# First tile's q and k loaded in 1 KB runs and turned by 64x64 products, the last kept sum seeded into PSUM, and a new order

## The chip, the cores and the metric

The kernel runs on one core of a Trainium2 chip. The metric is the device time of one execution in microseconds, the median of several runs; smaller is better. The profile is of one execution, and its times count from the start of its span.

## The reference

Attention in chunks of 64 tokens over 8 batches, 8 heads, 576 tokens and 64 features per head, then a feed-forward block over the 4608 tokens with 512 model and 2048 hidden features. All is float32:

```
scores = (q_c @ k_c.T) / 8                     # per chunk of 64 tokens
attn   = exp(scores - max) / (sum + 1e-9)
out    = attn @ v_c
x = out, heads beside each other               # 4608 x 512
h = x @ w_in                                   # 512 x 2048
g = h if h >= 1, 0 if h <= -1, else (h + 1)^2 / 4
y = g @ w_out                                  # 2048 x 512
```

## The kernel before, in words

The tokens are worked on in nine tiles of 512: the first 512 tokens of each batch, and one tile (the seventh) of the last 64 tokens of all eight. Heads are taken in pairs, four pairs (g = 0 to 3) per tile. Every FFN product is made of three products in the chip's reduced float32 form: high part of x with high and low part of the weight, and low part of x with the high part (`ffn_in`, L777; `ffn_out`, L813; each block of 128 hidden features is 12 products of 512 columns for either). The weights are loaded in 16 blocks for either matrix and split into high and low parts on the chip (`prepare`, L431: three operations on ACT, L442, L445 and L467, two on DVE, L450 and L471).

The first three tiles use the plain form, block by block. The tiles from the fourth on go two by two through a fast scheme for products of 2x2 blocks, with seven products in place of eight (`ffn_quad`, L1115; `ffn_mixed_out`, L1159). It needs mixed weights, which `mix_weights` (L883) makes while the first three tiles run and which POOL's queue writes to DRAM and streams back.

**Head.** Tile 0's attention is done pair by pair. `load_heads` (L527) loads q and k of a pair through `load_rows` (L485): two issues, one per head, in runs of 256 bytes, one token's features each; SP's queue issues them, and ACT's for k of pairs 0 and 1 (L537). A 128x512 tile then holds 64 tokens of a chunk on 64 partitions, for two heads. `attn_turn` (L551) turns it by four 128x128 transposes on PE (`flip`, L544) into a PSUM bank, and ACT copies it to SBUF (L560). `scores_of` and `values_of` (L569, L586) make 32 products of 64x64 each; `attn_softmax` (L647) takes the maximum (L658), subtracts it (L661), takes the exponential on ACT (L664), the sum and its reciprocal on DVE (L669 to L671) and multiplies on POOL (L674). `attn_turn_back` (L678) turns the result by `flip` again, with an ACT copy (L684). `attn_split` (L728) makes the high part xh on ACT (L737) and the low part xl on DVE (L738).

While PE has nothing ready in this head, the planner puts in warm-up products of the identity matrix, `warm` (L1472), until the first FFN product.

**Later pairs.** From tile 1 on, attention goes by two pairs at once in bursts (`burst`, L1390): 128-byte-run loads (`load_blocks`), 32x32 turns on DVE (L565), `attn_softmax_pair` (L686) and four DMAs that swap blocks of the turned result (`move`, L717). `PAIRS` (L1369) lists after which blocks of the first three tiles a burst is placed, `SCHEDULE` (L310) after which blocks, counted from the start, a mix of weights is placed and which scratch it uses.

**Order.** What each engine does is not written down as such: every operation is given to a planner (`Plan.add`, L87) with its engine, an assumed cost, what it reads and writes, and for loads their size and run. `Plan.run` (L153) plays this through as a list scheduler: an engine takes the ready operation of lowest rank. After each of two rounds the ranks are replaced by due times that are counted back from the end (`deadlines`, L123). The third pass writes the instructions in that order, so each engine's stream is fixed beforehand. `first_loads` (L1308) and `load_more` (L1334) give the loads' first ranks.

**Tail.** The last step of the last tile, `ending` in `ffn_mixed_out` (L1192), makes its products in two halves of tokens, e = 0 and 1, and two chunks of features, c = 0 and 1, into four half banks (`last_product`, L1150). They go into a pair of banks for e = 0 that attention used, `a_banks`, and `h_banks` for e = 1. `store_last` (L1222) adds on DVE the sum kept in D (`total_of`, L1065), turns it by 32x32 on DVE (L1239, L1242), and SP's and ACT's queues store it (L1248). Elsewhere (L1182) a kept sum is instead copied by ACT into PSUM, `seeded` (L1077), and the products add to it.

## Time and profile before

| | |
|---|---|
| median of three runs | 792.53 us (792.34 to 794.37) |
| the profiled execution | 793.6 us, its span 791.8 us |
| granted TensorE clock over the span | 0.999 |
| busy: PE, DVE, ACT, POOL | 782.8, 659.9, 523.4, 178.4 us |
| moved by DMA | 177.16 MB, 224 GB/s on average |

How to read it: the span runs from the first instruction to the last; the execution's own time is 1.8 us more than that. PE is TensorE's products (PEld its weight loads beside them), DVE VectorE, ACT ScalarE, POOL GpSimd, SP the engine that only issues DMAs; SPq, ACTq are the queues' issuing instructions. In the timeline a row is one instruction, or several alike in a row with their count (x4), with start, duration, engine, line of the kernel, output <- input, and in brackets the idle time before it and what ended it. A product's duration is from its start to its modelled end, and products overlap, so a row of several is shorter than the sum of its parts.

### The profile page before, as it was taken

What the parts mean: (1) busy time and instruction counts of PE and PEld (TensorE: products, weight loads), DVE (VectorE), ACT (ScalarE), POOL (GpSimd) and SP (SyncE); (2) the same over time, 40 slices, a digit from 0 to 9 for tenths busy, and PEclk for the clock granted to TensorE, in tenths of its full rate; (3) what the DMA queues carried; (4) which work ended last, traced back from release to release, by engine and by line L of the source; (5) the groups of instructions that cost most, each with busy time, mean ns of one, the idle gap of its engine ahead of it and who ended that gap; (6) DMA issues with size and microseconds to landing.
All of it is one profiled execution on the core that took longest, in us unless ns stands there. A gap on an engine that the chain in (4) does not pass through costs nothing.

```text
span 791.8 us, 15101 instructions
## 1 busy us (share of the span) xinstructions
PE 782.8 (99%) x5626; PEld 646.2 (82%) x5626; DVE 659.9 (83%) x1013; ACT 523.4 (66%) x903; POOL 178.4 (23%) x294
## 2 busy tenths in 40 slices
PE   9999999999999999999999999999999999999997
PEld 8788888878878888887887888888888888888886
DVE  4889998898679889998769999887699976755796
ACT  5998975444445456886579667865797658657851
POOL 1000005743234433222111112121112111211211
PEclk9999999999999999999999999999999999999999
DMA  9896869858799867898899879989766896666664
GB/s 207 221 359 152 252 136 289 290 174 234 190 277 278 219 170 232 246 299 229 225 243 240 225 210 271 273 226 241 204 198 185 220 260 207 191 192 191 183 207 106
DMA packets 254664, 177.16 MB, mean 224 GB/s; under 512 B 211968, under 2 KB 220160, under 8 KB 254592
## 3 DMA queue, kind: packets, MB, share of 16 engines
q0 software_dynamic: 33344, 117.98, 47.4%
q1 hardware_dynamic: 216992, 57.18, 32.0%
q10 hardware_dynamic: 4256, 1.05, 0.7%
q8 instruction: 44, 0.72, 0.4%
q14 instruction: 28, 0.23, 0.1%
HBM read 133.17 MB, written 38.80 MB: 217 GB/s over the span
## 4 chain that ended last, share of the span: by engine, by line
PE 83%; DVE 7%; ACT 4%; DMA 3%; SPq 1%; issue 1%; ACTq 0%; DVEq 0%
PE ps_o L1060 39%; PE ps_o L823 14%; PE ps_h L788 14%; PE ps_h L1060 12%; PE ps_a L579 2%; DMA aT_both<-qT_both 2%; PE ps_h L600 1%; DVE big_wo L1111 1%; DMA k_sb_both<-in_k_dram 1%; ACT big_wo L1110 1%; ACT big_wo L1107 1%; DMA words_wi<-in_moe_w_in_dram 1%; SPq L490 1%; SPq L722 0%; PE ps_o L600 0%
## 5 line engine op out<-in xcount | busy, mean ns | idle before, releaser
L968 POOL DMA_DIRECT2D big_wi<-mixed x144 | 76.8, 534 | 325.7 <-PE ps_o L1060 178.2
L788 PE MATMUL ps_h<-xh,parts_wi 128*128 128x512 f32 x376 | 123.9, 392 | 0.1
L823 PE MATMUL ps_o<-parts_wo,gh 128*128 128x512 f32 x384 | 119.5, 392 | 0.0
L1060 PE MATMUL ps_o<-big_wo,big_wi 128*128 128x512 f32 x396 | 95.6, 389 | 0.0
L1060 PE MATMUL ps_o<-gh,big_wi 128*128 128x512 f32 x264 | 88.6, 391 | 0.4 <-ACT big_wo L1075 0.3
L1060 PEld LDWEIGHTS ps_o<-big_wo,big_wi 128*128 128x128 f32 x396 | 74.3, 188 | 15.5
L788 PEld LDWEIGHTS ps_h<-xh,parts_wi 128*128 128x128 f32 x376 | 70.6, 188 | 16.5 <-DVE r L799 1.2
L823 PEld LDWEIGHTS ps_o<-parts_wo,gh 128*128 128x128 f32 x384 | 71.4, 188 | 15.3 <-issue 0.3
L1060 PE MATMUL ps_h<-big_wi,big_wi 128*128 128x512 f32 x312 | 75.9, 390 | 0.0
L823 PE MATMUL ps_o<-parts_wo,gl 128*128 128x512 f32 x192 | 74.8, 390 | 0.0
L788 PE MATMUL ps_h<-xl,parts_wi 128*128 128x512 f32 x188 | 73.3, 390 | 0.1
L1060 PE MATMUL ps_o<-big_wi,big_wi 128*128 128x512 f32 x282 | 70.8, 391 | 0.7 <-ACT tmp L1075 0.4
L1060 PEld LDWEIGHTS ps_h<-big_wi,big_wi 128*128 128x128 f32 x312 | 58.4, 188 | 12.2
L1167 ACT CAST big_wo<-big_wo 128x512 fp32r<-128x512 f32 x76 | 47.2, 622 | 31.6 <-PE ps_o L1060 19.9
L1060 PEld LDWEIGHTS ps_o<-big_wi,big_wi 128*128 128x128 f32 x282 | 52.6, 188 | 12.8 <-ACT tmp L1075 1.3
L1167 ACT CAST gh<-big_wo 128x512 fp32r<-128x512 f32 x76 | 47.2, 621 | 23.2 <-PE ps_o L1060 18.2
L1168 DVE TENSOR_TENSOR big_wo<-big_wo,big_wo 128x512 fp32r<-128x512 f32 x76 | 51.6, 684 | 11.6 <-ACT big_wo L1167 11.6
L1110 ACT ACTIVATE big_wo<-big_wo 128x512 f32<-128x512 f32 x96 | 59.8, 632 | 1.9
L1060 PEld LDWEIGHTS ps_o<-gh,big_wi 128*128 128x128 f32 x264 | 49.5, 188 | 12.0 <-ACT big_xl L753 0.8
L1168 DVE TENSOR_TENSOR gl<-big_wo,gh 128x512 fp32r<-128x512 f32 x76 | 51.6, 683 | 8.6 <-ACT gh L1167 8.5
L795 ACT ACTIVATE r<-ps_h 128x512 f32<-128x512 f32 x47 | 28.1, 597 | 36.4 <-PE ps_h L788 36.2
L1060 PE MATMUL ps_o<-gl,big_wi 128*128 128x512 f32 x132 | 51.4, 390 | 0.0
(269 smaller groups left out, 1648.9 us busy)
## 6 DMA issues: line engine op xcount, KB each, us to landing
big_wi<-mixed POOLq DMA_DIRECT2D x144, 512.0 KB, 4.7
big_wo<-mixed POOLq DMA_DIRECT2D x24, 512.0 KB, 4.3
words_wi<-in_moe_w_in_dram SPq DMA_DIRECT2D x16, 512.0 KB, 7.0
words_wo<-in_moe_w_out_dram SPq DMA_DIRECT2D x16, 512.0 KB, 8.8
v_sb<-in_v_dram SPq DMA_DIRECT2D x60, 128.0 KB, 4.0
q_sb_both<-in_q_dram SPq DMA_DIRECT2D x112, 64.0 KB, 3.9
k_sb_both<-in_k_dram SPq DMA_DIRECT2D x112, 64.0 KB, 3.1
mixed<-parts_wi POOLq DMA_DIRECT2D x24, 256.0 KB, 4.2
```

The costliest lines, as they stand in the source:

```text
L490: queue.dma_start(out=dst[j * C:(j + 1) * C], in_=heads_rows(src, t, 2 * g + j).rearrange("c p d -> p c d"),)
L579: nc.tensor.matmul(out=scores[i * C:(i + 1) * C, half, n * C:(n + 1) * C], lhsT=qT[rows, at], rhs=kT[rows, at], start=True, stop=True,)
L600: nc.tensor.matmul(out=values[half][h * C:(h + 1) * C, n * C:(n + 1) * C], lhsT=v_sb[rows, of:of + C], rhs=rhs, start=True, stop=True,)
L788: nc.tensor.matmul(out=ps, lhsT=weight["wi", j][:, half, kc * P:(kc + 1) * P], rhs=x(), start=(kc == 0 and i == 0), stop=(kc == KC - 1 and ...
L795: plan.add("act", 0.48, lambda: nc.scalar.activation(out=r, in_=ps, func=AF.Relu, bias=0.5, scale=0.5), (pkey,), (rkey,))
L823: nc.tensor.matmul(out=acc, lhsT=x[:, cols], rhs=weight["wo", j][:, half, :], start=(j == 0 and i == 0), stop=(j == NF - 1 and i == 2),)
L968: nc.gpsimd.dma_start(out=place_of(tag).bitcast(F32), in_=mixed[n][:, rows, :])
L1060: nc.tensor.matmul(out=bank, lhsT=parts[part], rhs=rhs, start=fresh and begin and k == 0, stop=end and k == 2, skip_group_check=not fresh,)
L1107: plan.add("act", 0.5, lambda: nc.scalar.activation(out=r(), in_=h(), func=AF.Relu, bias=0.5, scale=0.5), (hkey,), (rkey,))
L1110: plan.add("act", 0.52, lambda: nc.scalar.square(out=r(), in_=r()), (), (rkey,))
L1167: plan.add("act", 0.52, lambda: nc.scalar.copy(out=h(), in_=x()), (key,), (hkey,))
L1168: plan.add("dve", 0.6, lambda: nc.vector.tensor_tensor(out=l(), in0=x(), in1=h().bitcast(F32), op=ALU.subtract), (key, hkey), (lkey,))
```

## The change

**Loads.** `load_rows` makes one load per tensor and pair. Partition p now holds tokens 4p to 4p + 3 of either head, 256 numbers in a row, 1 KB. k of pairs 0 and 3 is issued by ACT, k of 1 by SP.

**Turns.** `flip_rows` makes 16 products of 64x64 with a part of the identity, each of which turns 64 partitions of one head and one of the four tokens, and writes the result into PSUM with a step of four words, so that the tokens are in order again. The upper half of the partitions now holds the first four chunks, the lower half the last four; the softmax writes its result in chunk order (`e4`).

**Engines.** `TURNED_BY`, `BACK_BY` and `NORM_BY` say who copies the turned q and k (two of eight on DVE, the others on ACT), who copies the turned-back result (all ACT) and who normalizes (all POOL).

**Products.** For the first four FFN-in blocks (`APART`) each product is given to the planner on its own, with only the parts that it reads.

**Planner.** ACT's queue of DMAs is modelled on its own. An operation of DVE with two inputs in SBUF, marked so, is not begun while a POOL operation runs: another ready one is taken, or it waits. Only the join and the low part in `prepare` are marked.

**Tail.** For the last step the kept sum D is copied by ACT into the four half banks before its products, and `store_last` turns straight from PSUM. The banks for e = 0 are `o_banks[2:]` instead of `a_banks`.

**Order.** `SCHEDULE`, `PAIRS`, the order of the w_out mixes, `first_loads` and the counts of `load_more` have other values.

```diff
-        self.queues = {"pool": deque(), "sp": deque()}
+        self.queues = {"pool": deque(), "sp": deque(), "act": deque()}
...
+            if e == "dve" and n in self.two_in_sbuf and start < port_free:
+                late = [n]
+                while now[e] and late[-1] in self.two_in_sbuf:
+                    late.append(heapq.heappop(now[e])[1])
+                n = late.pop() if late[-1] not in self.two_in_sbuf else late.pop(0)
+                for m in late:
+                    heapq.heappush(now[e], self.rank[m])
+                if n in self.two_in_sbuf:
+                    start = port_free
...
+            if e == "pool" and not sends:
+                port_free = end
...
-    EARLY = 2
+    EARLY, APART = 2, 4
+    ACT_LOADS = (('k', 0), ('k', 3))
+    TURNED_BY, BACK_BY, NORM_BY = "aaadadaa", "aaaa", "pppp"
...
-        (15, EARLIER), (15, EARLIER), (15, EARLIER), (17, EARLIER), (19, OWN), (22, EARLIER), (23, RING5), (25, RING5), (28, OWN), (33, OWN), (36, LATER), (39, LATER), (41, OWN), (41, RING5), (45, RING5), (46, OWN),
+        (15, EARLIER), (19, EARLIER), (19, RING5), (20, EARLIER), (21, RING5), (23, EARLIER), (25, EARLIER), (27, OWN), (27, OWN), (35, OWN), (37, LATER), (39, OWN), (40, LATER), (43, RING5), (44, OWN), (46, OWN),
...
-        plan.add("dve", 0.6, join, both, (ykey,))
+        plan.add("dve", 0.6, join, both, (ykey,), two_in_sbuf=True)
...
-        plan.add("dve", 0.6, low, (ykey, both[0]), (both[1],))
+        plan.add("dve", 0.6, low, (ykey, both[0]), (both[1],), two_in_sbuf=True)
...
-        dst = dst.rearrange("p (c d) -> p c d", d=D)
-        for j in range(2):
-            queue.dma_start(
-                out=dst[j * C:(j + 1) * C],
-                in_=heads_rows(src, t, 2 * g + j).rearrange("c p d -> p c d"),
-            )
+        rows = src[BATCH[t], 2 * g:2 * (g + 1), :T, :].rearrange("j (p r) d -> p j (r d)", p=P)
+        queue.dma_start(out=dst.rearrange("p (j f) -> p j f", j=2), in_=rows)
...
-            parts = 4 if load == load_blocks else 2
+            parts = {load_values: 2, load_rows: 1, load_blocks: 4}[load]
...
-            issuer, queue = ("act", nc.scalar) if (n, t) == ("k", 0) and g < 2 else ("sp", nc.sync)
+            issuer, queue = ("act", nc.scalar) if t == 0 and (n, g) in ACT_LOADS else ("sp", nc.sync)
...
+    def flip_rows(ps, src):
+        for j, r, half in itertools.product(range(2), range(NS), range(2)):
+            rows = slice(half * C, (half + 1) * C)
+            nc.tensor.matmul(
+                out=ps[rows].rearrange("p (n j b r) -> p j r n b", n=NS, j=2, r=NS)[:, j, r],
+                lhsT=src[rows, (j * NS + r) * D:(j * NS + r + 1) * D],
+                rhs=ident[rows, rows], start=True, stop=True,
+            )
...
+    def copied(by, to, bank):
+        (key, dst), (pkey, ps) = to, bank
+        if by == "d":
+            return plan.add("dve", 0.6, lambda: nc.vector.tensor_copy(out=dst, in_=ps), (pkey,), (key,))
+        return plan.add("act", 0.48, lambda: nc.scalar.copy(out=dst, in_=ps), (pkey,), (key,))
...
-            plan.add("pe", 0.45, lambda src=src, ps=ps: flip(ps, src), (skey,), (pkey,), columns=T)
-            turned[n] = plan.add(
-                "act", 0.48, lambda ps=ps, dst=dst: nc.scalar.copy(out=dst, in_=ps), (pkey,), (dkey,)
-            )
+            plan.add("pe", 0.55, lambda src=src, ps=ps: flip_rows(ps, src), (skey,), (pkey,), columns=T)
+            turned[n] = copied(TURNED_BY[2 * g + n], (dkey, dst), (pkey, ps))
...
-        e4 = e.rearrange("p (n h k) -> p h n k", h=2, k=C)
+        e4 = e.rearrange("p (h n k) -> p h n k", h=2, k=C)
...
+        engine, queue, cost = ("dve", nc.vector, 0.6) if NORM_BY[g] == "d" else ("pool", nc.gpsimd, 1.05)
+        plan.add(engine, cost, lambda: queue.tensor_tensor(
...
-        plan.add("act", 0.48, lambda: nc.scalar.copy(out=aT, in_=ps), (pkey,), (akey,))
+        copied(BACK_BY[g], (akey, aT), (pkey, ps))
...
+            def products(some, kc=kc, xh=xh, xl=xl):
+                for i in some:
+                    half, x = ((0, xh), (0, xl), (1, xh))[i]
...
-            plan.add("pe", 0.681, products, (f"wi{j}_0", f"wi{j}_1", hkey, lkey), (pkey,),
+            wkeys = [f"wi{j}_{half}" for half in range(2)]
+            if n < APART:
+                for i, reads in enumerate(((wkeys[0], hkey), (wkeys[0], lkey), (wkeys[1], hkey))):
+                    plan.add("pe", 0.227, lambda i=i, products=products: products((i,)), reads, (pkey,), columns=T)
+                continue
+            plan.add("pe", 0.681, lambda products=products: products(range(3)), (*wkeys, hkey, lkey), (pkey,),
                      columns=3 * T)
...
-    LAST_BANKS = a_banks, h_banks
-    LAST_SUMS = [whole(x) for x in (e_bufs[0], tmp_bufs[2])]
+    LAST_BANKS = o_banks[2:], h_banks
...
-            product(bank[:, :T // 2], parts, (h()[:, at], l()[:, at]), True, k == 0, k == PARTS - 1)
+            product(bank[:, :T // 2], parts, (h()[:, at], l()[:, at]), False, k == 0, k == PARTS - 1)
...
+            if ending:
+                for e, c in itertools.product(range(2), range(2)):
+                    key, x = chunks_of(D_TAG)[c]
+                    seeded(
+                        (LAST_BANKS[e][c][0], last_tokens(e, c)),
+                        (key, lambda x=x, e=e: x()[:, e * T // Q // 2:(e + 1) * T // Q // 2]),
+                    )
...
-    def store_last(t, h, e, sums):
-        (key, x), (okey, o) = LAST_SUMS[e], LAST_TURNED[e]
-        blocks = T // Q // 2
-        def chunk(x, c):
-            return x.rearrange("p (b c q) -> p c b q", c=2, q=Q)[:, c]
+    def last_tokens(e, c):
+        return LAST_BANKS[e][c][1][:, :T // 2].rearrange("p (b q) -> p b q", q=Q)
+    def store_last(t, h, e):
+        okey, o = LAST_TURNED[e]
         for c in range(2):
-            (skey, y), (bkey, bank) = sums[c], LAST_BANKS[e][c]
-            tokens = bank[:, :T // 2].rearrange("p (b q) -> p b q", q=Q)
-            total_of(
-                (f"{key}_{c}", lambda c=c: chunk(x(), c)), (bkey if e else LAST_BANKS[0][1][0], tokens),
-                (skey, lambda y=y: y()[:, e * blocks:(e + 1) * blocks]), None if e else last_turned[-1], 0.35,
-            )
-            if e:
-                plan.add("dve", 0.35, lambda c=c: nc.vector.transpose(out=chunk(o(), c), in_=chunk(x(), c)),
-                         (f"{key}_{c}",), (f"{okey}_{c}",))
-        if not e:
-            plan.add("dve", 0.63, lambda: nc.vector.transpose(out=o(), in_=x()),
-                     (f"{key}_0", f"{key}_1"), (f"{okey}_0", f"{okey}_1"))
+            plan.add("dve", 0.35, lambda c=c: nc.vector.transpose(
+                out=o().rearrange("p (b c q) -> p c b q", c=2, q=Q)[:, c], in_=last_tokens(e, c)
+            ), (LAST_BANKS[e][c if e else 1][0],), (f"{okey}_{c}",), after=None if e else last_turned[-1])
...
-        ("q", 0), ("k", 0), ("q", 1), ("k", 1), ("q", 2), ("k", 2), ("wi", 0), ("q", 3), ("k", 3),
-        ("v", 0), ("v", 1), ("wi", 1), ("v", 2), ("v", 3),
+        ("q", 0), ("k", 1), ("q", 1), ("k", 0), ("wi", 0), ("q", 2), ("k", 2), ("v", 3), ("v", 1), ("v", 2), ("q", 3), ("v", 0), ("k", 3), ("wi", 1),
...
-    load_more(5)
+    load_more(3)
     load_heads(1, 0, "qk")
-    load_more(0)
+    load_more(1)
     load_heads(1, 1, "qk")
-    load_more(2)
+    load_more(4)
...
-    PAIRS = {0: (6, 10, 15), 1: (7, 11), 2: (0, 4, 9, 15)}
+    PAIRS = {0: (3, 10, 15), 1: (3, 12), 2: (0, 7, 11, 15)}
...
-        what = ("wi", m) if m < NF // 2 else ("wo", (1, 2, 4, 5, 6, 7, 0, 3)[m - NF // 2])
+        what = ("wi", m) if m < NF // 2 else ("wo", (2, 6, 4, 0, 7, 3, 1, 5)[m - NF // 2])
```

## Rows read from the trace of the kernel before

**Rows 1.** The page, part 1: busy us (share of the span) xinstructions.

```profile
PE 782.8 (99%) x5626; PEld 646.2 (82%) x5626; DVE 659.9 (83%) x1013; ACT 523.4 (66%) x903; POOL 178.4 (23%) x294
```

**Rows 2.** Waits of PE from 35 us on: us in total, times, longest us.

```profile
PE ps_h L600 <- DVE r L799: 1.3, 2, 1.1
```

**Rows 3.** Groups of PE's instructions, 6 to 45 us: busy us, mean ns.

```profile
L1473 PE MATMUL ps_h<-ident 128*128 128x128 f32 x53 | 7.3, 277 | 0.0
```

**Rows 4.** Timeline of the head.

```profile
0.74 3.06 SPq L490 DMA_DIRECT2D q_sb_both<-in_q_dram  x4
...
6.15 0.63 PE L547 MATMUL ps_o<-ident,k_sb_both 128*128 128x128 f32 x4
...
8.04 0.69 PE L579 MATMUL ps_a<-kT_both,qT_both 64*64 64x64 f32 x32
...
8.80 0.69 DVE L658 TENSOR_REDUCE mx_both<-ps_a 128x8 f32<-128x512 f32 x1 [8.80 <-PE ps_a L579]
...
10.48 1.42 SPq L418 DMA_DIRECT2D words_wi<-in_moe_w_in_dram  x1
...
15.29 0.68 ACT L442 ACTIVATE tmp<-words_wi 128x512 f32<-128x512 f32 x1 [0.26 <-DMA words_wi<-in_moe_w_in_dram]
...
18.40 1.83 PE L1473 MATMUL ps_h<-ident 128*128 128x128 f32 x14
...
19.26 1.26 DVE L471 TENSOR_TENSOR parts_wi<-tmp,parts_wi 128x512 fp32r<-128x512 f32 x1
...
21.05 0.67 DVE L738 TENSOR_TENSOR xl<-ps_a,xh 128x512 fp32r<-128x512 f32 x1
...
21.81 0.50 PE L788 MATMUL ps_h<-xh,parts_wi 128*128 128x512 f32 x1
...
27.74 0.50 PE L788 MATMUL ps_h<-xh,parts_wi 128*128 128x512 f32 x1
...
28.85 0.69 DVE L738 TENSOR_TENSOR xl<-ps_o,xh 128x512 fp32r<-128x512 f32 x1 [0.35 <-ACT xh L737]
```

**Rows 5.** Stretches: busy us of PE, PEld, DVE, ACT, POOL; clock, DMA share, GB/s.

```profile
5.00:10.00 5.00, 4.89 (x69) 4.54 (x69) 1.16 (x2) 1.72 (x4) 0.00 (x0) 1.00 1.32 224
5.00:30.00 25.00, 24.50 (x393) 21.14 (x393) 17.45 (x32) 18.93 (x35) 4.17 (x4) 1.00 1.06 261
...
20.00:25.00 5.00, 4.73 (x87) 3.81 (x86) 4.93 (x9) 4.86 (x9) 1.04 (x1) 1.00 0.98 297
```

**Rows 6.** Timeline of the tail.

```profile
771.24 1.10 ACT L1081 COPY ps_o<-big_wo 128x512 f32<-128x512 f32 x2
...
779.25 0.65 DVE L1069 TENSOR_TENSOR big_wo<-ps_o,big_wo 128x512 f32<-128x512 f32 x1
...
781.08 1.40 DVE L1270 STREAM_TRANSPOSE big_wo<-ps_o 128x512 f32<-128x512 f32 x2 [1.18 <-PE ps_o L1060]
...
781.56 0.88 PE L1060 MATMUL ps_a<-big_wo,big_wo 128*128 128x256 f32 x6
...
787.44 0.42 DVE L1069 TENSOR_TENSOR tmp_both<-ps_h,big_wo 128x256 f32<-128x256 f32 x1 [0.51 <-PE ps_h L1060]
787.90 0.45 DVE L1239 STREAM_TRANSPOSE tmp<-tmp_both 128x256 f32<-128x256 f32 x1
```

**Rows 7.** A stretch of the first tile, columns as in rows 5.

```profile
80.00:100.00 20.00, 20.00 (x208) 16.57 (x207) 18.78 (x28) 19.75 (x37) 0.00 (x0) 1.00 0.88 248
```

**Rows 8.** The chain of waits, 200 to 240 us: start us, us, what.

```profile
200.66 2.72 PE ps_h L788 x12
...
225.18 0.73 SPq L722
...
227.97 6.35 DMA aT_both<-qT_both
```

**Rows 9.** Timeline of DVE in a later softmax.

```profile
409.84 1.22 DVE L697 TENSOR_REDUCE mx_both<-ps_a 128x16 f32<-128x1024 f32 x1
...
416.94 1.24 DVE L724 STREAM_TRANSPOSE qT_both<-kT_both 128x1024 f32<-128x1024 f32 x1
```

17 lines of the change are left out of this document (9 added, 8 removed).

## Prediction

> **What bounds the kernel now.** I read the page's busy times first, then PE's waits, then the head and the tail as timelines, then busy time by stretches. PE is busy for 782.8 us, 99% of the span [rows 1], and from 35 us to the end one kind of wait alone costs it over half a microsecond in all: 1.3 us before value products [rows 2]. So what can be won lies at the two ends, and in work of PE that is no work: from 6 to 45 us it spends 7.3 us on 53 warm-up products of L1473 [rows 3].
>
> The head runs as follows [rows 4]. SP begins with q and k of the first tile, four issues in 3.06 us, and reaches the first weight block at 10.48; ACT begins to convert it at 15.29. The first turn stands at 6.15, the first scores at 8.04, and DVE has nothing to do until 8.80. The first FFN product is at 21.81, right behind the subtraction that makes xl (21.05 + 0.67), though PE had run 14 warm-up products from 18.40. From 27.74 on PE goes from product to product without filler; the last xl of the tile ends at 29.54 (28.85 + 0.69). In between DVE sets the pace: it works 17.45 us between 5 and 30, all of it after 8.80, and 4.93 of the 5 us from 20 to 25 [rows 5]. One of its subtractions takes 1.26 us beside a POOL multiplication, where others of its size take 0.67 to 0.69 [rows 4].
>
> At the other end the last product ends just before 787.44; then follow a sum (0.42), a turn (0.45), the stores and their landing [rows 6].
>
> **The change, part by part.**
>
> *Loads of 1 KB runs.* Eight loads of 256 KB go from two issues each to one. SP has twelve such issues ahead of the first weight block now; at 3.06 / 4 = 0.77 us each [rows 4], six fewer are worth 4.6 us, and the new order puts the weights before the fourth pair besides. ACT issues two instead of four (k of the first and the last pair); k of the second pair joins SP's queue ahead of the weights, one issue of 0.77 us. On the wires the eight are 2.1 MB. From 5 to 10 us they move at 224 GB/s; from 20 to 25, where weights in longer runs are among the loads, the rate is 297 [rows 5]. So 9.4 us become 7.1, or stay. I take 297, since the weights' 1 KB runs are the nearest row: the first pair, 0.5 MB in 1.8 instead of 2.3 us and one issue less before its last part, is there 1.2 us sooner, the weights some 4 us sooner.
>
> *Turns by 64x64 products.* A turn is four transposes in 0.63 us now, and becomes 16 products of 64x64. The 32 score products take 0.69, and use all four quadrants: 0.69 / 8 = 0.086 for a group of four [rows 4]. The turn uses two quadrants. As dense as the scores, 16 take 0.35; if a pair takes a group's time, 0.69; if each product does, 1.4. I take 0.7, the middle case, since two can stand side by side. On PE that hides behind the 7.3 us of fillers. On the way to the first scores two longer turns cost 0.15, with what follows them 0.3.
>
> *Copies of turned tiles to DVE.* Two of eight. DVE gains 1.4 us (0.69 each, as its subtraction from PSUM at 28.85 [rows 4]), ACT loses 1.1 (0.55 each, as its copies of that size at 771.24 [rows 6]).
>
> *DVE and POOL kept apart.* The planner now makes a DVE operation with two SBUF inputs give way, or wait, while POOL multiplies. The 1.26 instead of 0.69 costs 0.57, and there are two of these in the head, 1.1 us. Waiting can cost as much: the bounds are 0 and 1.1, I take 0.8, since DVE has other operations to put in.
>
> *First four FFN-in blocks in single products.* PE can take xh with the high weights before xl and the low half are there. At most the 14 fillers from 18.40, 1.8 us, become work, at least none; I take 0.7, since xl follows xh by one operation of DVE.
>
> *Sum of the head.* DVE works 17.45 us in the 21.2 from 8.80 to 30 and idles 3.75 [rows 5]. After: start at 7.6, 1.2 sooner; work 17.45 + 1.4 - 0.8 = 18.05; idle 1.9, half of what it was, as weights and later pairs no longer come late. It ends at 27.55 instead of 30, 2.5 us sooner. With 0.7 for single products and less 0.3 for the turns that is 2.9. The 4 us sooner that the weights come also let ACT convert them in its gaps, 6.1 us from 5 to 30 [rows 5]; for that I add a small part, 0.5: **3.4 us**.
>
> *Bursts and mixes moved.* Nine attention bursts and sixteen mixes as before, in other places. The work is the same, and PE's products cover it. At best the 1.3 us of waits go [rows 2]; what could come is priced among the rivals. I take 0.
>
> *The kept sum seeded.* Four DVE sums of 128x256 go (0.42 each). The turns read PSUM, where two of 128x512 take 1.40 at 781.08, so 0.35 for half the size: not more than the 0.45 that one from SBUF takes at 787.90. On the path lies the last sum and its hand-over, 787.44 to 787.90: 0.46 [rows 6]. Added are four ACT copies into PSUM of half the size of those at 771.24, 0.3 to 0.55 each. The cover: the kept sum's last part ends at 779.90 and the last block's first product stands at 781.56, so 1.7 us for two copies of 1.1 at most. If it is gone, PE waits at most for four copies, 2.2. I take no wait: **0.5 us**.
>
> **Sum:** 3.4 + 0.5 = 3.9 us. The profiled execution took 793.6 us with a span of 791.8; the median of the three runs is 792.53, 1.1 below. The difference holds for both: 789.7 for an execution like the profiled one, and **788.6** against the median.
>
> **The rivals.**
>
> *ACT paces the first tile.* From 80 to 100 us ACT is busy 19.75 of 20 us [rows 7]. If it cannot begin the weights much sooner, PE's lead ends in waits between 40 and 110 us, and what stays is the 1.1 us moved to DVE and the tail: 1.6, or **790.9**. Against it speak ACT's 6.1 us of gaps before 30 us. That 1 KB runs move no faster than those of 256 B, so that the loads don't do what they should, ends near the same place: the shorter queue and the tail are then left.
>
> *More than I take.* Fillers give 1.8 instead of 0.7, waits of 0.8 go, DVE's idle time falls by 1.0 more: 3.9 + 2.9 = 6.8, **785.7**. For it speaks that all q and k can be there before DVE has done its second pair.
>
> *Slower: a burst's chain no longer fits between two bursts.* Bursts four blocks apart stand four times in the new list (15 to 19, 28 to 32, 39 to 43, 43 to 47 in blocks from the start), three times in the old. A block is two runs of 12 products, 2.72 us each, so four blocks are 21.8. The chain: four swaps issued and landed, 225.18 to 234.32 [rows 8], softmax and turn, 409.84 to 418.18, and the next turn, 1.24 [rows 9]: 9.1 + 8.3 + 1.2 = 18.7. It decides from 3.1 us of queueing on DVE, ACT and SP; 2.5 us more at three of the four places give 7.5 - 3.9 = 3.6 slower, **796.1**. For it: the wait of rows 2 stands behind such a swap. Against: the planner emits a burst when its inputs are ready, not at the listed block.
>
> *Slower: the turns themselves.* They write PSUM with a step of four words, which no row shows. If a turn takes f, eight add 8 (f - 0.63) to PE; the fillers give 7.3 us of room, and the head's gain 3.4 more. From f = 2.0 on that is spent; at f = 2.5, four times today's turn, it is 15.0 - 10.7 - 0.5 = 3.8 slower, **796.3**. The Trainium skill (PSUM — Partial Sum Buffer, Specifications (TRN2)) says that any non-contiguous pattern slows matmuls significantly; by that rule this case would be the likely one. It gives no factor, and no row here has a product that writes with a step.
>
> **How the numbers follow.** Forecast 0.57 (787.0 to 790.1 by the bounds of its terms), more 0.13, ACT's pace or loads no faster 0.20, the burst chain 0.06, the turns 0.04. A measurement of this kernel can tell about 0.3%, 2.4 us, from no change: faster is below 790.15, slower above 794.9. The first two cases are faster, 0.70, the third is the same, 0.20, the last two are slower, 0.10. The range, 785.5 to 792.6, takes in the first three down to no gain at all; outside are the slower two and the far end of the second.
>
> **What would show it.** Right: the first weight block issued by 6 us and in conversion by 12; DVE's first reduction before 8; turns of 0.5 to 0.9 us; fewer fillers; PE without filler from about 24.3; the last turn straight behind the last product, and the span's end 0.5 us closer to it. Wrong: new PE waits on ACT or DVE from 40 to 110 us (ACT's pace); turns over 1.4 us; PE waiting before value products in tiles two and three; a product of the last block waiting on an ACT copy. The forecast falls if PE's filler-free run starts after 26.5, or if its waits behind that grow by over 2 us.

## The result, and the profile after

| | before | after |
|---|---|---|
| median, us | 792.43 (791.36 to 794.37, 6 runs) | 797.59 (796.35 to 800.26, 6 runs) |
| the profiled execution, its span | 793.6, 791.8 | 797.36, 795.6 |
| first 512-column product | 21.81 | 24.10 |
| last product to the span's end | 4.40 | 5.19 |

The ratio is 1.0066 (95% interval 1.0046 to 1.0086): slower by 5.2 us, where 3.9 less was forecast. I compare executions by the start of PE's k-th product of 512 columns, counted from 0; both kernels have the same 3144 of them. Product 100 stands at 49.41 us before and is **4.84** later after; the last such product, number 3143, is 2.97 later; from there to the span's end it is 10.47 us before and 11.26 after, 0.79 more. So 4.84 are lost in the head, 1.87 come back in the middle, 0.79 are lost in the tail: 3.76, the difference of the two spans. Where a burst's own products stand at other places of this count, the shift jumps by 1.4 us and jumps back behind them; I read it clear of such places, and say so where product 100 lies in one.

PE's busy time, from the page of the kernel after, answers [rows 1]:

```profile
PE 784.0 (99%) x5826; PEld 648.5 (82%) x5826; DVE 658.3 (83%) x1012; ACT 523.3 (66%) x905; POOL 178.4 (22%) x294
```

PE is still the bound; the span grew by 3.8 us and PE's busy time by 1.2. The head after, as a timeline, answers [rows 4]:

```profile
4.38 0.37 SPq L436 DMA_DIRECT2D words_wi<-in_moe_w_in_dram  x1
...
6.36 1.66 PE L568 MATMUL ps_o<-ident,k_sb_both 64*64 64x64 f32 x32
...
7.86 1.10 PE L568 MATMUL ps_o<-ident,q_sb_both 64*64 64x64 f32 x32
...
10.39 0.27 PE L608 MATMUL ps_a<-kT_both,qT_both 64*64 64x64 f32 x1
...
10.79 0.69 DVE L579 COPY first_wo<-ps_o 128x512 f32<-128x512 f32 x1 [10.79 <-PE ps_o L568]
...
11.40 0.68 DVE L686 TENSOR_REDUCE mx_both<-ps_a 128x8 f32<-128x512 f32 x1
...
14.40 1.00 PEld L568 LDWEIGHTS ps_o<-ident,first_wi 64*64 64x64 f32 x31 [0.95 <-ACT e L692]
...
16.08 0.67 ACT L460 ACTIVATE tmp<-words_wi 128x512 f32<-128x512 f32 x1
...
18.38 0.19 PEld L568 LDWEIGHTS ps_o<-ident,first_wi 64*64 64x64 f32 x2 [0.54 <-issue]
...
24.10 0.48 PE L818 MATMUL ps_h<-xh,parts_wi 128*128 128x512 f32 x1
...
25.14 0.75 PEld L1502 LDWEIGHTS ps_o<-ident 128*128 128x128 f32 x6 [0.53 <-issue]
```

A turn is sixteen products, but 32 records: an fp32 product of 64x64 stands in the trace as two. (The 32 records of a scores row, which take 0.69, are sixteen products as well, and the counts of warm-up products in the rows are records too, two to a product.) A turn takes 1.10 us at the full clock, against 0.63 for four transposes, and the first 1.66, since the granted clock rose at 7.52 us only (before at 5.03; PE had warm-up products in front in both). So part of the 4.84 is this execution's late clock: in the run without a step, below, with the same order and the clock up at 5.72, product 100 is at +2.97. Scores begin at 10.39 instead of 8.04, DVE's first reduction at 11.40 instead of 8.80. The first weight block is issued 6 us sooner, yet ACT converts it 0.8 us later. PE now waits three times in mid-stream, before 14.40, 18.38 and 25.14.

Stretches, to answer [rows 5]; the columns are those of the line that begins with "core 0: us":

```profile
core 0: us, PE busy (x) PEld busy (x) DVE busy (x) ACT busy (x) POOL busy (x), PEclk, DMA share, GB/s
5.00:10.00 5.00, 5.00 (x91) 4.59 (x92) 0.00 (x0) 1.17 (x2) 0.00 (x0) 1.00 1.06 350
5.00:30.00 25.00, 23.18 (x545) 20.48 (x544) 14.75 (x30) 14.13 (x26) 4.36 (x4) 1.00 0.89 246
```

From 5 to 10 us the loads move 350 GB/s where 224 were moved before [rows 5]. All eight are issued by 3.75 us. The first pair's q, issued at 0.74, lands 3.3 us later; before, the second half of q was issued at 1.6 and took 4.8:

```profile
L507 SPq DMA_DIRECT2D q_sb_both<-in_q_dram x1: 447/447/447, 0.7 to 0.7; - x1
DMA to landing us min/median/max: 3.3/3.3/3.3
...
L490 SPq DMA_DIRECT2D q_sb_both<-in_q_dram x2: 763/808/854, 0.7 to 1.6; - x2
DMA to landing us min/median/max: 3.8/4.3/4.8
```

(the first two lines are the kernel after, the last two the kernel before). With k, the pair is complete at 4.36 instead of 6.39, 2.0 us sooner, but PE turns it at 6.36 only: in PE's fixed order 22 records of warm-up products stand in front, and at half the clock they last until 6.2. DVE did 14.75 us of work up to 30 us instead of 17.45.

PE's waits, to answer [rows 2]:

```profile
PE ps_o L858 <- DVE tmp L878: 1.6, 1, 1.6
...
PE ps_o L568 <- issue: 1.2, 2, 0.8
```

The 1.3 us before value products are gone; a new wait of 1.6 stands at 139 us, before the FFN-out products on the way from tile 0 to tile 1, behind DVE's copy of a result out of PSUM. That copy (138.72) stood behind a burst's turn, before which DVE had been idle for 3.8 us:

```profile
137.56 1.25 DVE L594 STREAM_TRANSPOSE qT_both<-q_sb_both 128x1024 f32<-128x1024 f32 x1 [3.79 <-DMA out_dram<-tmp]
...
L886 SPq DMA_DIRECT2D out_dram<-tmp x1: 897/897/897, 134.3 to 134.3; - x1
DMA to landing us min/median/max: 4.0/4.0/4.0
...
L751 SPq DMA_DIRECT2D aT_both<-qT_both x4: 524/920/1159, 130.6 to 133.1; - x4
DMA to landing us min/median/max: 3.7/4.4/4.7
```

The bracket names a store, but that store, issued at 134.33, landed at 138.28, when the turn was already running. What landed last before 137.56 is the last of the four swaps of the burst in front, which read qT_both: issued at 133.07, landed at 137.48. So, as far as the landings tell, this burst's turn waited for the swaps of the burst before it.

The tail, to answer [rows 6]:

```profile
781.48 0.37 ACT L1115 COPY ps_h<-big_wo 128x256 f32<-128x256 f32 x1
781.57 0.69 DVE L1103 TENSOR_TENSOR big_wo<-ps_o,big_wo 128x512 f32<-128x512 f32 x1 [0.50 <-ACT ps_o L1115]
...
782.78 1.24 DVE L1304 STREAM_TRANSPOSE big_wo<-big_wo 128x1024 f32<-128x1024 f32 x1
...
784.31 2.62 POOL L1314 DMA_DIRECT2D out_dram<-big_wo  x4 [12.61 <-DVE big_wo L1304]
...
790.47 0.45 DVE L1271 STREAM_TRANSPOSE tmp<-ps_h 128x256 f32<-128x256 f32 x1 [1.03 <-PE ps_h L1094]
```

The last turn does stand right behind the last product, without a sum between, and ends 0.4 us sooner, measured from the last 512-column product (6.62 us behind it instead of 7.01). The last store lands 9.52 us behind that product, before 9.54: no later. What ends later is the closing operation of POOL's queue, a DRAIN:

```profile
L1508 POOLq DRAIN  x3: 40/102/7525, 781.0 to 791.5; - x3
...
L1537 POOLq DRAIN  x3: 40/102/9072, 785.7 to 795.3; - x3
```

(before, then after). Its longest took 7.53 us and ended 7.21 behind that product before; after, it took 9.07 and ended 10.48 behind it, when SP's queue had been done for 0.6 us. POOL's four stores are issued 1.7 us later, counted in the same way, because the turn that they store (782.78; before 778.09) now stands behind a sum that waits for ACT's seed (781.57) and a low part. Why the DRAIN itself is 1.5 us longer, no row shows.

### The profile page after: what moved, and what is told of

Its sections match the earlier page's. It is cut to its first block, busy times and chain, and to the rows that moved or that the text cites. A ratio compares the mean times of both kernels' runs of the same rounds, so it can differ in the third digit from the quotient of the medians.

```text
span 795.6 us, 15498 instructions
## 1 busy us (share of the span) xinstructions
PE 784.0 (99%) x5826; PEld 648.5 (82%) x5826; DVE 658.3 (83%) x1012; ACT 523.3 (66%) x905; POOL 178.4 (22%) x294
## 4 chain that ended last, share of the span: by engine, by line
PE 81%; DVE 12%; ACT 3%; DMA 1%; issue 1%; SPq 1%; POOL 0%; DVEq 0%; ACTq 0%; POOLq 0%
PE ps_o L1094 33%; PE ps_o L858 16%; PE ps_h L818 15%; PE ps_h L1094 10%; PE ps_a L608 2%; DVE big_wo L1145 2%; PE ps_h L629 1%; PE ps_h L1502 1%; DVE big_wo L1103 1%; DVE gl L1202 1%; PE ps_o L568 1%; DVE big_wo L1119 1%; DVE big_wo L1202 1%; DVE big_wi L1074 1%; DMA aT_both<-qT_both 1%
```

## The experiments

Four theories at the start. T: the turns are too long, and stand in PE's order ahead of the scores. L: eight loads share the wires, so the first pair is no sooner (the landings above speak against it: 4.36 instead of 6.39). O: the new places of bursts and mixes cost in the middle. S: the seeds put the end off. Later I (PE waits for its own instructions) and A (ACT paces the first tile) joined them. "Shift" is the start of a 512-column product against the profiled execution before.

### Old turns in the kernel after

```diff
-            plan.add("pe", 0.55, lambda src=src, ps=ps: flip_rows(ps, src), (skey,), (pkey,), columns=T)
+            plan.add("pe", 0.55, lambda src=src, ps=ps: flip(ps, src), (skey,), (pkey,), columns=T)
```

> The changed kernel with each turn made by four 128x128 transposes again; loads, order of every engine and everything else stay as changed. q and k reach the scores with their tokens and features in other places, so the output is another one; the work per instruction is the same. Theory T (the turns are the loss: 16 products of 64x64 in 32 records take 1.08 us where four transposes take 0.63): the head is back, the 512-column products come about 4 us sooner than in the changed kernel, 100 products in within 1 us of the kernel before; time 793 to 794, ratio to the kernel before 1.000 to 1.002. Theory L (all eight loads share the wires, the first pair is no sooner and the head waits on loads): under 1.5 us gained, 796 to 797.5. Theory O (the new order of engines is the loss): under 1 us gained, 796.5 to 797.5.

Measured: 793.12 us, ratio 1.0001 (0.9982 to 1.002). (The transposes set rows of other tokens together: another computation of the same size.) Every engine's order is that of the kernel after, so the difference is the turns alone: the shift of product 100 goes from +4.84 to -1.18, 6.0 us, and the time by 4.5. The middle gives less back in the profiled execution (shift +2.39 at the end): PE waits 2.1 us each at 133.8 (again behind a burst's swap) and 408.9, and the clock falls to half for 3.4 us behind either. That execution, 796.74 us, is the slowest of ten, so its middle is not typical of the 793.12.

### Old loads in the kernel after

```diff
-        rows = src[BATCH[t], 2 * g:2 * (g + 1), :T, :].rearrange("j (p r) d -> p j (r d)", p=P)
-        queue.dma_start(out=dst.rearrange("p (j f) -> p j f", j=2), in_=rows)
+        dst = dst.rearrange("p (c d) -> p c d", d=D)
+        for j in range(2):
+            queue.dma_start(
+                out=dst[j * C:(j + 1) * C],
+                in_=heads_rows(src, t, 2 * g + j).rearrange("c p d -> p c d"),
+            )
```

> The changed kernel with q and k of the first tile loaded in 256-byte runs by two issues each; turns, order of the other engines and the rest stay as changed. Tokens come to other places than the turns assume, so the output is another one. Theory T: loads are not what the head waits for, and slower ones cost what the first pair comes later, 0 to 2 us: 797.5 to 799.5. Theory L: loads in flight together are the loss, whatever their run, so the time stays within 1 us of the changed kernel; with the four issues of ACT's and SP's queues spread out as before the first pair could even come sooner. If 1 KB runs are worth what was forecast, 2 to 3 us slower: 799.5 to 801.

Measured: 799.21 us, ratio 1.0079 (1.006 to 1.0097); shift of product 100 +3.53. (Here too other tokens meet.) The head is 1.3 us better without the new loads (its clock rose at 4.6 us, that of the kernel after at 7.5), the end 1.9 worse, by waits of PE at 138, 390 and 516 us. With two clocks that differ by 3 us, the two heads don't tell what the loads are worth; the run with the loads alone, below, tells more.

### Old tail in the kernel after

```diff
-                    store_last(t + last[2], last[1], e)
+                    store_last(t + last[2], last[1], e, chunks_of(last[0]))
```

(and `store_last`, `last_product` and the banks as before; no seeds)

> The changed kernel with the tail of before: no kept sum seeded, the sum on DVE, attention's banks for the first half. Head and middle are the changed kernel's, instruction by instruction. From the last product to the span's end the changed kernel takes 5.2 us, the kernel before 4.4. Theory S (the seeding holds up the sum behind it and the stores of the tile before, which then collide with the last stores): 4.4 again, 0.8 us faster than the changed kernel, 796.7. Rival (the longer end is chance, the landing of single stores): the sum and its turn come back to the path, 0.4 to 0.5 slower, 798.

Measured: 797.18 us, ratio 1.0053 (1.0037 to 1.007); from the last 512-column product to the end 10.44 us, as before (10.47), against 11.26. In the profiled executions this end takes 11.15 to 11.26 us in the seven kernels with four seeds, 10.43 to 10.47 in the eight without them. So the seeds, with the other banks that come with them, cost the tail 0.8 us; seeds and banks are not told apart, and the time itself, 0.4 better, does not show it.

### Old layout in the kernel after

Loads, turns, places of the chunks and the planner's figures for them as before; order, engines and tail as after.

```diff
-            parts = {load_values: 2, load_rows: 1, load_blocks: 4}[load]
+            parts = {load_values: 2, load_rows: 2, load_blocks: 4}[load]
...
-            plan.add("pe", 0.55, lambda src=src, ps=ps: flip_rows(ps, src), (skey,), (pkey,), columns=T)
+            plan.add("pe", 0.45, lambda src=src, ps=ps: flip(ps, src), (skey,), (pkey,), columns=T)
...
-        e4 = e.rearrange("p (h n k) -> p h n k", h=2, k=C)
+        e4 = e.rearrange("p (n h k) -> p h n k", h=2, k=C)
```

> The changed kernel with loads in 256-byte runs, transposes and the old place of chunks, and with the planner told so: all else of the change (copies on DVE, single products, planner's rule, order, tail) stays. Theory T: the head is as before or better, 100 products in within 1 us of the kernel before or up to 2 us sooner, and with what the changed kernel gains between 40 and 300 us (1.9 us) the time is 790.5 to 793. Theory O: no better than 796.

Measured: 799.17 us, ratio 1.008 (1.0063 to 1.0097): a miss. The head is nearly that of before (+0.64 at product 100), but PE then waits 1.7 us at 136 (a burst's swap again), 2.5 at 282, 0.9 at 344 and 0.9 at 515. The waits at 282 and 344 are put down to "issue": of their kind more below.

### The layout alone in the kernel before

```diff
-            plan.add("pe", 0.45, lambda src=src, ps=ps: flip(ps, src), (skey,), (pkey,), columns=T)
+            plan.add("pe", 0.55, lambda src=src, ps=ps: flip_rows(ps, src), (skey,), (pkey,), columns=T)
```

(with `load_rows` and `e4` of after)

> The kernel before with the layout of the first tile's q and k alone: one load of 1 KB runs each, turns by 64x64 products, softmax's view to match; order, engines and tail stay as before. Theory T (turns of 1.08 us ahead of the scores in PE's stream pace the head): PE's 512-column product number 100 stands 3 to 5 us later than before, and after what the middle gives back the end is 2.5 to 4.5 us later, 795 to 797. Rival L (fewer issues put the weights and later pairs forward, and that outweighs the turns when the order is the old one): product 100 no later than 1 us, 791 to 793.5.

Measured: 797.99 us, ratio 1.0075 (1.006 to 1.009); product 100 at +4.36 (in a burst's place; +5.74 at products 40 to 80 and from 160 on), the last at +4.46. The layout by itself loses what the whole change loses, though its clock rose at 4.34 us and the first turn is 0.95 us sooner (5.20). PE's weight loads in its timeline:

```profile
10.18 1.02 PEld L550 LDWEIGHTS ps_o<-ident,first_wi 64*64 64x64 f32 x32
11.26 0.52 PEld L1480 LDWEIGHTS ps_h<-ident 128*128 128x128 f32 x4
11.90 0.19 PEld L550 LDWEIGHTS ps_o<-ident,first_wi 64*64 64x64 f32 x2
13.06 0.89 PEld L550 LDWEIGHTS ps_o<-ident,first_wi 64*64 64x64 f32 x28 [0.97 <-issue]
...
15.48 1.03 PEld L550 LDWEIGHTS ps_o<-ident,first_wi 64*64 64x64 f32 x32
18.33 0.52 PEld L1480 LDWEIGHTS ps_h<-ident 128*128 128x128 f32 x4 [1.82 <-issue]
...
23.72 0.64 PEld L1480 LDWEIGHTS ps_h<-ident 128*128 128x128 f32 x5
25.16 0.41 PEld L1480 LDWEIGHTS ps_h<-ident 128*128 128x128 f32 x3 [0.80 <-issue]
```

A turn is broken off after two of its 32 records, and nothing that the profile shows is waited for: 3.6 us in three waits. Counting PE's records (weight loads and products) from the start of the trace, the three waits stand behind numbers **444, 699 and 953**: 255 and 254 apart. In the kernel after the three waits stand behind the same three numbers (13.37, 17.70 and 24.42 us there; the first of them is put down to ACT by the profile), and so do those found with the old order, the turns without a step and the old tail (all three) and with the old loads (699), whatever the time. The instruction queue brings its loads in 16 KB each, and the waits end 1.2 to 1.6 us after the packets of one have moved: in this run the packets end at 11.70, 16.80 and 23.67. The number of loads fits: before, 11,252 records of PE and 44 loads, after, 11,652 and 46, 256 and 253 records to a load. So theory I: PE has run to the end of the instructions that it has. The longer waits put down to "issue" behind the head are of the same kind, in every kernel: 2.1 us at 408.9 with the old turns, 2.5 at 282 with the old layout, 1.5 at 500.6 with the warm-up products in pieces, 0.3 at 498.6 in the kernel before, all end 1.3 to 1.6 us after a load's packets. When a load is asked for, and so why it is late here and not there, no run shows.

### The old order in the kernel after

```diff
-    PAIRS = {0: (3, 10, 15), 1: (3, 12), 2: (0, 7, 11, 15)}
+    PAIRS = {0: (6, 10, 15), 1: (7, 11), 2: (0, 4, 9, 15)}
```

(and `SCHEDULE`, the order of w_out mixes and the counts of `load_more`)

> The kernel after with the old places of mixes and bursts (SCHEDULE, PAIRS, which wo block is mixed when, how many weight loads stand between those of tile 1); layout, head engines and tail as after. Theory T: the head's shift stays at +4.5 to +5 us at product 100, and the time is within 1.5 of the kernel after's, 796 to 799. Rival O (the new order makes the 1.8 us stall near 139 us and the others, and is worth 2 us and more): stalls of PE behind 36 us sum to 2 us or less, and the time is 793.5 to 795.5.

Measured: 800.54 us, ratio 1.0102 (1.008 to 1.0123). Neither expectation: the stall at 139 us is gone, as O said, but others come, 2.2 us at 332 before scores (put down to issue, 1.3 to 1.6 us after a load's packets like those above; the clock then falls for 3.4 us) and 0.8 at 518. The head's shift is +3.8 at products 40 to 80 and +2.42 at product 100, in a burst's place; the last product's is +6.64. With the new layout the new order is 2.9 us better than the old, but the executions spread from 797.36 to 803.06, and the wait at 332 with the fall of the clock is not the doing of bursts and mixes.

### The true price of a turn in the planner

```diff
-            plan.add("pe", 0.55, lambda src=src, ps=ps: flip_rows(ps, src), (skey,), (pkey,), columns=T)
+            plan.add("pe", 1.08, lambda src=src, ps=ps: flip_rows(ps, src), (skey,), (pkey,), columns=T)
```

> The kernel after with one number changed: the planner reckons a turn by 64x64 products at 1.08 us, what the trace shows, instead of 0.55. Theory T in the form that the turns of the second pair delay the first scores only because the planner thinks them short: the first scores and DVE's first reduction come 1 us or more sooner than in the kernel after (10.4 and 11.4), product 100 stands at +3 to +4 instead of +4.8, and the time is 795.5 to 797. Rival (the turns cost their time wherever they are put): product 100 within 0.5 of +4.8 and the time within 0.8 of 797.6.

Measured: 806.47 us, ratio 1.0177 (1.0161 to 1.0194). The scores do come sooner (8.61 instead of 10.39), the first reduction at 9.56, and then all is lost: with the new price the planner leaves seven records of warm-up products after 5 us instead of 43, PE stands still four times, 5.1 us in all, from 11.2 to 21.8, and the granted clock is at half from 22.23 to 32.47. Product 100 is at +11.75. A dearer entry changed what PE does while it waits; T in this form can't be told from it.

### Only the head's engines in the kernel before

```diff
+    EARLY, APART = 2, 4
+    ACT_LOADS = (('k', 0), ('k', 1))
+    TURNED_BY, BACK_BY, NORM_BY = "aaadadaa", "aaaa", "pppp"
```

(with `two_in_sbuf`, `port_free`, `copied` and the single products of after)

> The kernel before with the head's engine changes alone: two copies of turned tiles on DVE, DVE and POOL kept apart by the planner, the first four FFN-in blocks in single products; loads, turns, order and tail as before. Theory E (these are the parts that gain): product 100 stands 0.7 to 2 us sooner, the time is 790.5 to 791.8. Rival (they were only worth something beside the new loads): product 100 within 0.5 of before's, the time 791.9 to 793.

Measured: 791.67 us, ratio 0.9991 (0.9976 to 1.0007). The first 512-column product is 1.66 sooner, the two slow subtractions of 1.26 are gone, but product 40 stands at +0.15. The last is at -1.90, since PE's idle time behind 36 us is 1.8 us instead of 2.7 and some smaller losses go; over all runs that is no difference that can be told.

### Turns written without a step

```diff
-                out=ps[rows].rearrange("p (n j b r) -> p j r n b", n=NS, j=2, r=NS)[:, j, r],
+                out=ps[rows, (j * NS + r) * C:(j * NS + r + 1) * C],
```

> The kernel after with the same sixteen products of a turn, written to 64 neighbouring words of PSUM each instead of every fourth word. The columns of the turned tiles then stand in another order, so the tile's attention is another computation of the same size; nothing else changes. Theory T (a turn takes long because each fp32 product of 64x64 is run as two and only two of the four quadrants are used): a turn still takes 1.05 to 1.15 us at the full clock, product 100 is within 0.7 of +4.8, the time 796.5 to 798.5. Rival (the step of four words in PSUM slows the products): a turn of 0.55 to 0.8 us, product 100 at +2 or less, the time below 795.5.

Measured: 796.59 us, ratio 1.0048 (1.0032 to 1.0063).

```profile
6.08 1.15 PE L568 MATMUL ps_o<-ident,k_sb_both 64*64 64x64 f32 x32
7.07 1.10 PE L568 MATMUL ps_o<-ident,q_sb_both 64*64 64x64 f32 x32
```

1.10 us with neighbouring words, 1.10 with a step of four: the step costs nothing here. Product 100 is at +2.97, lower than expected; in this execution the clock rose at 5.72 us (first turn 1.15 instead of 1.66) and the three instruction waits were 0.50, 0.40 and 0.46 instead of 1.03, 0.67 and 0.72.

### The 1 KB loads alone in the kernel before

```diff
+        rows = src[BATCH[t], 2 * g:2 * (g + 1), :T, :].rearrange("j (p r) d -> p j (r d)", p=P)
+        queue.dma_start(out=dst.rearrange("p (j f) -> p j f", j=2), in_=rows)
```

(turns by `flip`)

> The kernel before with the 1 KB loads of the first tile's q and k alone; the turns stay four transposes of 128x128, whose results then don't go with the rest (rows of other tokens stand in each chunk: another computation of the same size). If the loads are worth what the forecast said and only the turns spoil it: the first turn at 5.2 to 5.6 (before 6.15), product 100 at -0.5 to -2, the time 790 to 791.8. Rival (the loads are hidden behind DVE's chain and bring nothing): product 100 within 0.4 of before's, the time 792 to 793.

Measured: 792.51 us, ratio 1.0001 (0.9988 to 1.0014). The first turn is at 5.80, the first 512-column product 2.44 us sooner, product 40 at +0.73; so it stays up to product 80 and from 160 on, and product 100, in a burst's place, is at -0.66. The clock rose at 6.57 here. The rival: what the loads gain is gone by 34 us.

### Warm-up products in four pieces

```diff
-            out=bank[:, :P], lhsT=ident, rhs=ident, start=True, stop=True
+            out=bank[rows, n * C:(n + 1) * C], lhsT=ident[rows, rows], rhs=ident[rows, rows],
+            start=True, stop=True,
```

(four times per warm-up product, for two halves of rows)

> The kernel before with each warm-up product of 128x128 replaced by four products of 64x64 on two quadrants: about as long (0.27 us at 0.034 per record), but four times the instructions, some 500 more on PE in the head, as many as the new turns add; no chain of work is longer. Theory I (the new turns also cost by their number of instructions: PE reaches the end of what is loaded, and waits): issue waits of 0.5 us and more on PE's weight loads before 27 us that the kernel before does not have, the third instruction load before 24 us (before 26.7), product 100 at +0.8 to +2.5. Rival (number is harmless, only the turns' length counts): no such wait, product 100 within 0.4 of before's.

Measured: 795.15 us, ratio 1.0033 (1.0014 to 1.0051); product 100 at +1.69. The third instruction load comes at 17.34, sooner than I expected, but in the head no wait for issue is longer than 0.28: the packets of the first three loads end at 9.50, 14.93 and 18.58, and PE comes to the three records at 10.96, 16.84 and 21.07, 1.4 us and more behind each. The loss may have a plainer reason, which is argued and not shown: four warm-up products take 1.07 us in pieces and 0.89 whole, in the way of turns behind them. So the number of instructions by itself does not make the waits; where PE comes late enough to the end of what it has, the load is there.

### Twice the transposes: as long, with few instructions

```diff
-            plan.add("pe", 0.55, lambda src=src, ps=ps: flip_rows(ps, src), (skey,), (pkey,), columns=T)
+            plan.add("pe", 0.55, lambda src=src, ps=ps: [flip(ps, src) for _ in range(2)], (skey,), (pkey,), columns=T)
```

(in the kernel before with the new layout's loads)

> The kernel before with the new layout's loads, and as a turn the four transposes of 128x128 issued twice over: as long on PE as a turn by 64x64 products (0.93 us from first weight load to the next turn's), with 8 more instructions a turn instead of 56. As in the run with the loads alone, the turned rows then don't go with the rest: another computation of the same size. Theory T (the layout costs by the length of its turns, which stand in PE's order ahead of scores): product 100 at +3 to +5.5 against before, near the +5.74 of the layout by 64x64 products, and the time 795 to 798. Rival I (the issue waits behind instruction loads, 3.6 us in all in the layout alone, are what costs): product 100 at +0.7 to +2.2, no issue wait above 0.5 us before 27 us, the time 792 to 794.5.

Measured: 794.65 us, ratio 1.0018 (1.0007 to 1.003); product 100 at +1.01 (in a burst's place; +2.39 at products 40 to 80 and from 160 on), the last at +1.17. PE's timeline:

```profile
7.17 1.04 PE L543 MATMUL ps_o<-ident,q_sb_both 128*128 128x128 f32 x8
...
8.49 1.04 PE L543 MATMUL ps_o<-ident,k_sb_both 128*128 128x128 f32 x8
9.46 0.69 PE L586 MATMUL ps_a<-kT_both,qT_both 64*64 64x64 f32 x32
```

The longest waits of PE's weight loads from 5 to 36 us:

```profile
PEld ps_h L795 <- DVE r L806: 1.1, 1, 1.1
PEld ps_o L607 <- ACT words_wi L445: 0.4, 1, 0.4
```

Turns of 1.04 us and no wait for issue above 0.17. This splits the layout's cost. Clear of the burst's place the shift is +0.73 with the loads alone, +2.39 with turns as long as the new ones, +5.73 with the new turns: **1.7 us are their length, 3.3 the rest**, and the three waits for instructions are 3.6. The clock rose at 6.82 here and at 4.34 with the new turns, which works against this difference. At product 100 the result lies within what I gave for I, clear of the burst's place just above it, far below T either way.

### Loads and engines together, without the new turns

```diff
-            parts = {load_values: 2, load_rows: 2, load_blocks: 4}[load]
+            parts = {load_values: 2, load_rows: 1, load_blocks: 4}[load]
```

(the kernel with the head's engines alone, and `load_rows` of after)

> The kernel before with the 1 KB loads and the head's engine changes together, turns as before (another computation of the same size, as in the run with the loads alone). Each part alone brought the first FFN product 1.7 to 2.4 us forward, and PE then waited near 33.5 us behind a DVE product that waited for ACT, which is busy 5.00 of 5 us from 30 to 35. Theory A (ACT paces the first tile): the first product is 3 us or more sooner, product 40 no sooner than -0.4, and the time 791.3 to 792.6. Rival (the gains add): product 40 at -1.5 or less, the time below 790.8.

Measured: 795.29 us, ratio 1.0025 (1.0012 to 1.0038). The first 512-column product is 3.27 us sooner, product 20 at -2.79, product 40 at -0.09. Its stretches:

```profile
25.00:30.00 5.00, 5.00 (x53) 3.88 (x53) 3.82 (x7) 5.00 (x11) 0.00 (x0) 1.00 1.07 390
30.00:35.00 5.00, 3.27 (x14) 2.38 (x14) 3.67 (x7) 5.00 (x10) 0.00 (x0) 1.00 0.72 120
```

The waits from 30 to 36 us:

```profile
PE ps_h L818 <- DVE r L834: 1.7, 1, 1.7
DVE r L834 <- ACT r L833: 1.3, 1, 1.3
```

ACT is busy 5.00 of 5 us in both stretches; PE, 2.8 us ahead, waits 1.7 us for a DVE product that waits for ACT. A is shown for this place: the lead ends where ACT cannot split weights and pass on results any faster. The time missed A's range: PE waits another 1.7 us near 85 and 91, on DVE's turn and xl there.

### The parts that had not lost

```diff
-            product(bank[:, :T // 2], parts, (h()[:, at], l()[:, at]), True, k == 0, k == PARTS - 1)
+            product(bank[:, :T // 2], parts, (h()[:, at], l()[:, at]), at.start == 0, k == 0, k == PARTS - 1)
```

(the kernel with the head's engines alone, with seeds and turns from PSUM for the second half of the tokens only)

> The kernel before with the parts that have not lost: the head's engine changes, and in the tail only the last two of the four kept sums seeded into PSUM, so that the last two turns read PSUM and the store of the first half stays as before. Theory: product 100 within 0.3 of before's, fewer and shorter waits of PE behind 36 us, and 0.3 to 0.5 us less from the last 512-column product to the end; 790.5 to 791.7. Rival (the seeds delay the first half's sum or the end as they do in the kernel after): last product to end 10.5 or more, the time 791.7 to 793.

Measured: 792.23 us, ratio 0.9993 (0.9982 to 1.0003). From the last 512-column product to the end 10.04 us instead of 10.47, close to the 0.46 that the forecast gave the tail; PE's idle time behind 36 us is 1.9. By the runs it cannot be told from the kernel before, so no version here beats that.

## Why the prediction was wrong

**Turns: the step that failed.** The prediction has "The 32 score products take 0.69 ... 0.086 for a group of four ... I take 0.7" and "with what follows them 0.3". The 32 are records of sixteen products, so the group of four products is 0.17, and by my own reasoning the middle case should have been 1.4; measured 1.10. The single records bear the middle case out: those of a turn start in twos, those of scores in fours, each group 58 ns behind the one before. That the step in PSUM has no part in it is shown too: 1.10 us with and without. The Trainium skill (TensorEngine Tiling (Array Packing), Restrictions and Gotchas) says that column tiling excludes the transpose mode for fp32 input; no run here tries the two together. The trace has one record for a 128x128 transpose and two for each 64x64 product of a turn. The Trainium skill's rule that I weighed as a rival (PSUM — Partial Sum Buffer, Specifications (TRN2)), that non-contiguous patterns slow matmuls significantly, is not borne out at this shape.

Worse was the 0.3. A turn's time does not hide behind warm-up products only because PE has 7.3 us of them: turns stand in PE's fixed order in front of scores, which all of DVE's work in the head follows. And I counted instructions for the DMA queues, but none for PE: eight turns add 56 records each, weight loads and products together, and PE ran out of them three times. Together the turns cost 5.0 us around product 60 in the old order (5.74 against 0.73 with the loads alone) and 6.0 in the new one: 1.7 of the 5.0 are their length, 3.3 the rest, where the three waits for instructions are 3.6.

**Loads.** "The first pair is there 1.2 us sooner": it landed 2.0 us sooner, but nothing behind it gained as much. The first turn is 0.95 sooner with the layout alone, 0.35 with the loads alone and in the kernel after not at all, because PE's order is fixed and warm-up products stand in front of it. The rate was better than my 297 (350 GB/s). "The weights 4 us sooner" was 6.1 at the issue and nothing at the conversion, which ACT does in its order behind copies of the late turns.

**DVE's idle time halves, 2.5 us.** The loads and the engines together bring the first product 3.3 us forward where turns are short. In the kernel after, DVE begins at 11.40 instead of 7.6 and works 14.75 us up to 30, so its idle time did not halve. And the next limit was close by: from 25 to 35 us ACT is full, and by product 40 nothing was left. The rival "ACT paces the first tile", to which I gave 0.20, was right about that, only its place was 30 to 35 us, not 40 to 110.

**Products, DVE and POOL apart.** Both did what they should (the subtractions of 1.26 became 0.7 in the kernel with the engines alone; 43 records of warm-up products from 5 to 45 us in the kernel after instead of 67), and are worth nothing measurable for the same reason.

**Order.** I took 0, and the runs do not settle it. With the new layout the new order is 2.9 us better (800.54 against 797.59), with the wait and the fall of the clock at 332 us in it. With the old layout it is worse: the kernel after with the old layout takes 799.17, of which 0.8 is the tail, the one with the engines alone 791.67. PE's idle time behind 36 us is 6.3 us in the one and 1.8 in the other; of the difference 3.4 are the two waits for instructions at 282 and 344; the wait behind the swap at 136 is 1.7. With the new loads and the old turns, last, the new order takes 793.12 (ratio 1.0001, 0.9982 to 1.002) and the old 795.29 (1.0025, 1.0012 to 1.0038), though these two differ in seeds and the order of the first loads too. The burst rival named the right wait, at its first place (15 to 19): in all seven kernels with the new places of bursts, the turn of the later burst of that pair begins 0.1 to 0.2 us after the last swap of the one in front has landed (137.56 after 137.48 in the kernel after, 131.96 after 131.88 with the old turns). It costs PE 1.6 us in the kernel after, at this one place, not 2.5 at three, so the rival was not what made the kernel slower.

**Tail.** The 0.5 on the last sum is real (0.43 in the last run). The four seeds, or the banks that came with them, cost 0.8 net all the same: the last store lands no later, but POOL's DRAIN, which the prediction does not have, takes 9.07 instead of 7.53 us and becomes the end. I looked for a wait of PE there.

Of the rivals "the turns themselves" had the right sign and nearly the right place, but "from f = 2.0 on" was wrong: at f = 1.1 it already decided.

## What to carry to other kernels

Where an operation is replaced by many small ones, count its instructions on its own engine: a dense run of small products outruns the loading of instructions, and shows as waits without a releaser that stand behind the same records in one variant after the other. Time hidden behind filler work is only hidden if nothing in the chain stands behind it in the engine's order. An earlier head is worth what the next engine lets through: look, before pricing a gain, for the first stretch behind it in which some engine is busy all the time. And hold the releaser that a profile names against its own landing: the store named before DVE's turn at 137.56 us landed 0.7 us after that turn had begun.

## What the runs showed of the hardware

- PE waits for its instructions: loads of 16 KB, waits behind records 444, 699 and 953, each ending 1.2 to 1.6 us after a load's packets. The profile's page counts the loads, 44 before and 46 after:

```profile
q8 instruction: 46, 0.75, 0.4%
```

- 32 records of 64x64 fp32 take 1.10 us on two quadrants (turns) and 0.69 on four (scores): 58 ns to each two, and to each four, of them. A step of four words in PSUM changes nothing (1.10 us).
- The granted clock first rose between 4.3 and 7.5 us from run to run, with warm-up products from the start in all; a first turn that began at half clock took 1.66 us, one at the full clock 1.15. It fell again for 3.4 us behind waits of 2.1 to 2.2 us (old turns, old order), not behind one of 2.5 (old layout, at 282 us), and for 10.2 us where PE had stood still for 5.1 of the 11 us before.
- A burst's swaps landed in 3.7 to 4.7 us at 131 us, and in 6.35 at 228 us in the kernel before [rows 8]. POOL's closing DRAIN took 7.5 us before and 9.1 after.
